# The last mode of the weights by another queue, and the last jobs dealt out earlier

## The chip, the cores and the metric

One core of a Trainium2 chip runs the whole program. The metric is the device time of one execution in microseconds (us), the median of several runs. Lower is better.

## What is computed

The first half is causal attention with a sliding window of 64, for 8 batches of 8 heads, 576 positions and 64 channels a head. The second half takes its result `x` (8 x 576 x 512) through a spectral mix and a projection:

```python
X = np.fft.rfft(x, axis=1)
Xr, Xi = np.real(X[:, :64]), np.imag(X[:, :64])
Yr = np.einsum('bmd,mde->bme', Xr, w_r) - np.einsum('bmd,mde->bme', Xi, w_i)
Yi = np.einsum('bmd,mde->bme', Xr, w_i) + np.einsum('bmd,mde->bme', Xi, w_r)
Y[:, :64] = Yr + 1j * Yi
y = np.fft.irfft(Y, n=576, axis=1)
u = x + y
out = u + np.maximum(u @ w_ch, 0.0)
```

All inputs are fp32. `w_r` and `w_i` have a 512 x 512 matrix for each of 64 modes: 134 MB together, which must all be read.

## The kernel before

**Weights.** GpSimd's queue loads the weights and converts fp32 to bf16 on the way. One load is four modes, one half of the input channels (`hb`) and one of `w_r` and `w_i` (`ri`): 128 partitions, four rows of 4 KB each in fp32, 1 MB when it has landed. `wlist` (L105 to L114) holds the order of all loads; `load_weights` (L142) issues the next ones whenever a buffer is free that `mode_half` has marked as `spent`. In the last stage the buffers are three tiles of `ringA`. The very last load is cut in three transfers, of two modes, one and one, so that products can begin before all of it has landed.

**Products by mode.** `mode_half` (L176) multiplies one load with the spectrum of `x`: eight or sixteen small matmuls at L188. In the last load (`ending`) they go mode by mode, in the order of landing. The order of the groups is written out in `steps`; the last two are `LAST` and `LAST + 1`, and the groups after number 9 are done while the loads of the second stage run, from about 200 us.

**Jobs under the loads.** Between two `mode_half` calls, TensorE works through a list of `jobs`, each of which `advance` (L613) takes in two halves: prepare, and done one call later. The first jobs multiply the transposed `x` by `w_ch` (L603, L610). When the group ahead of `LAST` is finished, 36 more are appended: `batch_job` (a batch's rows of Y: transposes at L688, products at L610), `early_u` (the inverse transform of rows that can be started without the last two groups, L715 and L716) and `add_late` (L703). `want` says how many jobs are to have been given after each `mode_half`. In the last eight halves it rises by 36 in six steps; before the last two halves all that is left is worked off.

**The tail.** When the last load has been multiplied, `finish_group` evicts its result (L627, L628), turns it (L648), and a chain of products (L1007, L1015) leads to the rows of the output: `early`, `full_u`, `full_z` and `last`, each with a buffer of `new_ut`. Its first buffer, `utx`, is 128 x 2 x 512 fp32 in a pool of its own (`utpool`, opened at L946 when the last stage starts), taken at the first use; the others are tiles of `ringA`. GpSimd adds for some rows (L835), SP and ACT send them out.

**SP's queue** has two loads at the start (L356), eight copies of a few rows of the inverse table within SBUF (`trigL` at L951, `trigLr` at L952), which the tail reads, and the output.

Of the kernel before, what the change touches and what calls it, by code (L numbers as in the profile page):

```python
# [9 lines left out]
FP32 = mybir.dt.float32  # L10
# [16 lines left out]
def kernel(  # L27
# [10 lines left out]
    nc = tc.nc  # L38
    B, H, S, D = q.shape
    NM = moe_w_r.shape[0]  # L40
    DM = moe_w_ch.shape[0]
# [7 lines left out]
    HALF = DM // 2  # L49
    NJ = 2  # L50
# [5 lines left out]
    def pool(name, bufs=1, **kw):  # L56
        opened.append(tc.alloc_tile_pool(name=name, bufs=bufs, **kw))
        return opened[-1]

    def close(*pools):  # L60
        for x in pools:
            opened.remove(x)
            x.release()

    NLB = 4
# [38 lines left out]
    wlist = []  # L104
    for at, (grp, hb) in enumerate(steps):  # L105
        for ri in range(2):
            p = 4 * grp
            if (at, ri) == ONES:
                parts = [[(p, p + 1)], [(p + 2,)], [(p + 3,)]]
            elif (at, ri) == (len(steps) - 1, 1):  # L110
                parts = [[(p, p + 1), (p + 2,), (p + 3,)]]
            else:
                parts = [[(p, p + 1, p + 2, p + 3)]]
            wlist += [(at, part, hb, ri) for part in parts]  # L114
# [15 lines left out]
        lent.update((wstart[at] + i, t) for i, t in enumerate(of))  # L130
    lentY = Yall.rearrange("p (g j) e -> p g j e", j=NJ)
    NLY = 1
    wtiles, spent = {}, set()
    held = {"a": [], "b": [], "y": []}
    room = {"a": NRA, "b": NRB, "y": NLY}
    nload = 0
# [5 lines left out]
    def load_weights(n):  # L142
        nonlocal nload
        while nload < len(wlist):
            at, parts, hb, ri = wlist[nload]
            if 2 * n <= sum(len(ps) for ps in parts):
                return
            if nload in lent:
                w = lent[nload]
            else:  # L150
                open_to = "a" if at >= 2 * EARLY else "aby" if at < EARLY + 2 else "ab"
                h = min(open_to, key=lambda h: held[h][0] if len(held[h]) == room[h] else -1)
                if len(held[h]) == room[h]:
                    if held[h][0] not in spent:
                        return
                    held[h].pop(0)
                held[h].append(nload)
                if h == "y":
                    w = lentY
                else:  # L160
                    w = {"a": ringA, "b": ringB}[h].tile([128, 4, NJ, DM], BF16, name="wi" if ri else "wr", tag="wt")
            src = moe_w_i if ri else moe_w_r
            to = 0
            for ps in parts:
                nc.gpsimd.dma_start(  # L165
                    out=w[:, to:to + len(ps)],
                    in_=src[ps[0]:ps[-1] + 1, HALF * hb:HALF * hb + HALF, :].rearrange("g (p j) e -> p g j e", j=NJ))
                for i, p in enumerate(ps):
                    wtiles[p, hb, ri] = w[:, to + i]
                to += len(ps)  # L170
            nload += 1
            n -= to

# [21 lines left out]
    with tc.manual_schedule():  # L197
# [175 lines left out]
        at = scratch[:, 3 * NTF * NM:3 * NTF * NM + NTF]  # L373
# [104 lines left out]
        for it in range(-3, NU + 3):  # L478
# [23 lines left out]
            g = starts.get(it + 2)  # L502
# [3 lines left out]
            g = starts.get(it + 1)  # L506
# [35 lines left out]
        def bank(h, shape=(128, DM), dtype=FP32, name=None):  # L542
            return banks[h].tile(list(shape), dtype, name=name or "ps" + h, tag="bank")
# [69 lines left out]
        def advance():  # L613
            if jobs:
                prepare, done = jobs.pop(0)
                pend.append((prepare(), done))
                if len(pend) < 2:
                    return
            if pend:
                tr, done = pend.pop(0)  # L620
                done(tr)
# [108 lines left out]
        def early_jobs(b):  # L730
            early_u(b, (1,))
            add_late(b, 0)
            early_u(b, (3,))
            add_late(b, 1)
            add_late(b, 2)
            early_u(b, (0, 2))
            add_late(b, 3)
# [7 lines left out]
        NT = len(tiles)  # L745
# [6 lines left out]
        def x_jobs(pl, lo, hi):  # L752
            for i in range(lo, hi):
                def done(tr, i=i):
                    XW[i] = pl.tile([128, DM], FP32R, name=f"xw{i}")
                    nc.vector.tensor_copy(out=XW[i], in_=multiply(tr))  # L756
                jobs.append((lambda i=i: transposed(tiles[i][0]), done))
# [13 lines left out]
        ps, pu = {}, {}  # L771
# [11 lines left out]
        def tail_xw(n, js=(0, 1)):  # L783
            for i in [seq[n][j] for j in js]:
                ps[i] = bank("zt"[n % 2 == 0])
                nc.tensor.matmul(out=ps[i], lhsT=ident_r, rhs=XW[i], start=True, stop=True)  # L786
# [81 lines left out]
                nc.tensor.matmul(out=ps[i], lhsT=trigIr[:, at:at + 128], rhs=zrows(b), start=False, stop=True,  # L868
                                 skip_group_check=True)

        uts, homes = {}, []
        utpool, taken_uts = None, 0
        NUT = 2 * NRA + 1

        def new_ut():
            nonlocal taken_uts
            if not homes:
                homes.append(utpool.tile([128, 2, DM], FP32, name="utx"))
            elif taken_uts == len(homes) < NUT:
                t = ringA.tile([128, 4, DM], FP32, name="ut", tag="wt")  # L880
                homes.extend([t[:, 0:2], t[:, 2:4]])
            taken_uts += 1
            return homes[(taken_uts - 1) % NUT]
# [47 lines left out]
        NX0 = 10  # L931
        x_jobs(pool("xp0", reuse_waits="tile"), 0, NX0)
        psm = None
        half = given = 0
        n0, n1 = 2 * EARLY, 4 * (NGRP - EARLY)
        for i, (grp, hb) in enumerate(steps[EARLY:]):
            f, l = grp < EARLY or hb == 0, hb == 1
            if i == EARLY:
                while tables:
                    tables.pop(0)()  # L940
                while jobs or pend:
                    advance()
                close(stmp2, yp, ringB)
                Zall = pool("zall", side="right").tile([2 * NM, B, DM], FP32R, name="Zall")
                x_jobs(pool("xp1", side="right", reuse_waits="tile"), NX0, NT)
                utpool = pool("utpool", side="right", reuse_waits="tile")  # L946
                nc.vector.memset(YT[:, :, :, rows], 0.0)
                nc.vector.tensor_scalar(out=trz.rearrange("p c g k -> p c (g k)"), scalar1=0.0, scalar2=None, op0=ALU.mult,
                                        in0=ident.unsqueeze(1).to_broadcast([128, NDCH, 128]))
                for g in range(4):  # L950
                    nc.sync.dma_start(out=trigL[32 * g:32 * g + 16], in_=trigI[rows, 0:512])  # L951
                    nc.sync.dma_start(out=trigLr.bitcast(FP32)[32 * g:32 * g + 16], in_=trigIr.bitcast(FP32)[rows, 0:512])  # L952
                given = 0
            if f:
                psm = [bank("m"), bank("m")] if grp == LAST + 1 else bank("m")
            for ri in range(2):
                if half == n0 + n1 - 2:
                    while jobs or pend:
                        advance()
                if half == n0 + n1 - 1:  # L960
                    late["first"] = bank("z")
                    late[0][1]()
                    tail_xw(0)
                mode_half(psm, grp, hb, ri, f, l)
                load_weights(len(wlist))
                while ready:
                    ready.pop(0)()
                for t in tables[0:2]:
                    t()
                del tables[0:2]  # L970
                if half == 0:
                    nc.gpsimd.dma_start(out=wch, in_=moe_w_ch.rearrange("(c p) e -> p c e", p=128))
                if l and ri:
                    finish_group(grp, psm)
                    if grp == NGRP - 1:
                        ready.pop(0)()
                        for b in range(B):
                            batch_job(b)
                            if 0 < b <= NLB:
                                early_jobs(b - 1)  # L980
                half += 1
                if half <= n0:
                    want = max(half - 4, 0) * NX0 // (n0 - 4)
                elif half <= n0 + n1 - 8:
                    want = (half - n0) * (NT - NX0) // (n1 - 8)
                else:
                    want = NT - NX0 + (half - n0 - n1 + 8) * (B + 7 * NLB) // 6
                while given < want:
                    advance()
                    given += 1  # L990
# [74 lines left out]
```

## Time and profile before

| | |
|---|---|
| median of 3 runs | 435.25 us (435.19 to 435.46) |
| profiled execution | 434.85 us, span 433.1 us |
| TensorE matmuls (PE) | 322.2 us busy, 74% |
| VectorE (DVE), ScalarE (ACT), GpSimd (POOL) | 230.0, 179.9, 101.3 us busy |
| HBM read | 163.58 MB, 400 GB/s over the span |
| chain that ended last | DMA 50%, PE 36%, issue 6% |

The engines are named as in the table; PEld is TensorE's weight load, SPq and POOLq are the queues' issues. "L188" is line 188 of the kernel before. In a line of the profile, `psm<-wi,XL` means that the tile `psm` was written from `wi` and `XL`, and `<-` behind an idle time names what ended it. A transfer's sizes are those written, so a converted load counts half of what was read. Times in a trace are from the start of the span.

### The profile page before, as it was taken

Reading aid. Unit: us, or ns where it says so; the run is one execution under the profiler, and the core shown is the slowest. Engines: PE = TensorE matmul, PEld = TensorE weight load, DVE = VectorE, ACT = ScalarE, POOL = GpSimd, SP = SyncE. Lnnn points to the kernel's source line nnn. Section 1 sums busy time; section 2 is a strip of 40 time slices with the busy share of each in tenths; the row PEclk is TensorE's granted clock in tenths of the full one; section 3 lists DMA queues with packets and bytes.
Section 4 is the critical chain, followed back from the end, with each engine's and each line's share of the span. In section 5 each row is a group of like instructions: output and inputs, shape, how many; then the busy total and the mean of one; then the engine's idle time right before and its main releaser. Section 6 shows DMA issues by size and latency. Waiting matters only on the chain.

```text
span 433.1 us, 10990 instructions
## 1 busy us (share of the span) xinstructions
PE 322.2 (74%) x4758; PEld 216.0 (50%) x4802; DVE 230.0 (53%) x472; ACT 179.9 (42%) x322; POOL 101.3 (23%) x150
## 2 busy tenths in 40 slices
PE   6888899898999999962207353767564768789994
PEld 3666667576677677641104221444343445345652
DVE  8588787876776777863104111222131315653994
ACT  5665757666666666520201100122121213325842
POOL 8322222222131231131102100012111111110990
PEclk9999999999999999996557756588899889989998
DMA  8999999999999999999999999999999999993798
GB/s 210 211 211 212 211 212 212 210 211 212 212 213 210 211 212 212 212 212 212 211 259 213 217 212 212 212 212 212 212 212 212 212 211 211 212 211 72 243 367 295
DMA packets 47280, 93.64 MB, mean 216 GB/s; under 512 B 2688, under 2 KB 3136, under 8 KB 47232
## 3 DMA queue, kind: packets, MB, share of 16 engines
q0 software_dynamic: 41008, 81.73, 99.7%
q1 hardware_dynamic: 5328, 9.77, 6.6%
q10 hardware_dynamic: 896, 1.44, 0.9%
q8 instruction: 37, 0.61, 0.5%
q14 instruction: 11, 0.09, 0.1%
HBM read 163.58 MB, written 9.44 MB: 400 GB/s over the span
## 4 chain that ended last, share of the span: by engine, by line
DMA 50%; PE 36%; issue 6%; ACT 3%; DVE 2%; POOL 1%; DVEq 0%; POOLq 0%
DMA wi<-in_moe_w_i_dram 29%; DMA wr<-in_moe_w_r_dram 22%; PE tr L231 6%; PE s L278 4%; PE s L290 3%; PE pt L298 3%; PE psm L188 3%; PE vb L243 3%; PE o L318 2%; PE s L270 2%; PE pst L786 1%; PE psz L786 1%; PE psz L610 1%; PE pst L868 1%; PE px L341 1%
## 5 line engine op out<-in xcount | busy, mean ns | idle before, releaser
L610 PE MATMUL psz<-wch,tr 128*128 128x512 f32 x176 | 62.5, 488 | 11.3 <-DMA wch<-in_moe_w_ch_dram 11.0
L756 DVE CAST xw<-psz 128x512 fp32r<-128x512 f32 x36 | 24.9, 692 | 86.1 <-PE psz L610 86.1
L584 ACT CAST tr<-ptx 128x512 fp32r<-128x512 bf16 x36 | 21.1, 586 | 102.9 <-PE ptx L603 102.9
L282 DVE TENSOR_REDUCE mx<-s 128x4 fp32r<-128x512 f32 x72 | 49.5, 688 | 26.9 <-PE s L278 26.4
L188 PEld LDWEIGHTS <-XQ 128*32 128x32 bf16 x448 | 18.9, 174 | 78.3 <-issue 53.8
L165 POOL DMA_DIRECT2D wi<-in_moe_w_i_dram x32 | 23.4, 732 | 103.6 <-PE psm L188 70.2
L188 PE MATMUL psm<-wi,XQ 128*32 128x512 bf16 x208 | 19.8, 454 | 37.1 <-DMA wi<-in_moe_w_i_dram 37.1
L610 PEld LDWEIGHTS psz<-wch,tr 128*128 128x128 f32 x176 | 37.4, 235 | 18.4 <-issue 11.6
L292 ACT ACTIVATE p<-s 128x512 bf16<-128x512 f32 x72 | 39.7, 604 | 12.8 <-PE s L290 12.8
L165 POOL DMA_DIRECT2D wr<-in_moe_w_r_dram x27 | 20.3, 754 | 95.8 <-PE psm L188 77.8
L188 PE MATMUL psm<-wr,XQ 128*32 128x512 bf16 x184 | 18.6, 483 | 28.1 <-DMA wr<-in_moe_w_r_dram 27.2
L278 PE MATMUL s<-kT,qT 64*64 64x128 bf16 (+1 forms) x576 | 29.2, 222 | 6.7 <-issue 6.7
L235 ACT COPY kT<-tr 128x576 bf16<-128x576 bf16 x32 | 23.2, 724 | 20.2 <-PE tr L231 20.2
L235 ACT COPY qT<-tr 128x576 bf16<-128x576 bf16 x32 | 23.3, 729 | 10.6 <-PE tr L231 10.6
L301 DVE COPY pts<-pt 128x1024 bf16<-128x1024 bf16 (+1 forms) x40 | 25.2, 629 | 4.5 <-PE pt L298 3.1
L278 PEld LDWEIGHTS <-qT 64*64 64x64 bf16 x576 | 17.8, 107 | 17.9 <-issue 17.5
L290 PE MATMUL s<-mx,ident_r 128*128 128x512 f32 x72 | 26.2, 437 | 0.0
L635 DVE TENSOR_TENSOR stg<-psm,Yfour 128x512 bf16<-128x512 f32 x10 | 6.9, 689 | 36.3 <-PE psm L188 36.3
L235 ACT COPY vT<-tr 128x576 bf16<-128x576 bf16 x32 | 23.3, 728 | 4.1 <-PE tr L231 4.0
L298 PE MATMUL pt<-ident_bf,p 128*128 128x128 bf16 x288 | 23.3, 221 | 1.7 <-issue 1.6
L218 POOL DMA_DIRECT2D rawk<-in_k_dram x15 | 8.1, 540 | 66.0 <-PE tr L231 59.9
L330 DVE TENSOR_TENSOR x_sb<-o,r 128x512 bf16<-128x512 f32 x32 | 22.1, 691 | 1.1
(217 smaller groups left out, 598.3 us busy)
## 6 DMA issues: line engine op xcount, KB each, us to landing
wi<-in_moe_w_i_dram POOLq DMA_DIRECT2D x29, 1024.0 KB, 18.7
wr<-in_moe_w_r_dram POOLq DMA_DIRECT2D x27, 1024.0 KB, 17.7
out_dram<-ut SPq DMA_DIRECT2D x23, 256.0 KB, 2.8
rawv<-in_v_dram POOLq DMA_DIRECT2D x16, 288.0 KB, 14.9
rawk<-in_k_dram POOLq DMA_DIRECT2D x15, 288.0 KB, 13.9
rawq<-in_q_dram POOLq DMA_DIRECT2D x15, 288.0 KB, 13.8
x_sb<-in_moe_w_r_dram POOLq DMA_DIRECT2D x2, 1024.0 KB, 15.4
out_dram<-utx SPq DMA_DIRECT2D x5, 256.0 KB, 3.1
```

The costliest lines, as they stand in the source:

```text
L165: nc.gpsimd.dma_start(out=w[:, to:to + len(ps)], in_=src[ps[0]:ps[-1] + 1, HALF * hb:HALF * hb + HALF, :].rearrange("g (p j) e -> p g j e" ...
L188: nc.tensor.matmul(out=ps[32 * g:32 * g + 32, 0:e], lhsT=of.rearrange("k s b m -> k (s b) m")[:, (3 * j + 1 - ri) * B:(3 * j + 5 - ri) * B ...
L231: nc.tensor.transpose(out=pt[ro, j, :], in_=raw[ro, TH * half + j, :], identity=ident_bf[ro, ro])
L235: nc.scalar.copy(out=to, in_=pt.rearrange("p j n -> p n j"))
L278: nc.tensor.matmul(out=s[ro, t, lo:128], lhsT=lq, rhs=kT[ro, 64 * n - 64 + lo:64 * n + 64], start=False, stop=True, skip_group_check=True)
L282: nc.vector.tensor_reduce(out=mx, in_=s, axis=AX.X, op=ALU.max, negate=True)
L290: nc.tensor.matmul(out=s, lhsT=ident_r, rhs=mx.unsqueeze(2).to_broadcast([128, 4, 128]), start=False, stop=True, skip_group_check=True)
L292: nc.scalar.activation(out=p[:, 4 * c2:4 * c2 + 4, :], in_=s, func=ACT_F.Exp, scale=EX_SCALE)
L298: nc.tensor.transpose(out=pt[:, t, :], in_=st[u]["p"][:, t, :], identity=ident_bf)
L301: nc.vector.tensor_copy(out=ps[:, 0:nt, :], in_=pt[:, 0:nt, :])
L610: nc.tensor.matmul(out=pz, lhsT=tr[:, c, :], rhs=wch[:, c, :], start=(c == 0), stop=(c == NDCH - 1))
L756: nc.vector.tensor_copy(out=XW[i], in_=multiply(tr))
```

## The change

There are two parts. The last load, whose modes are `p` to `p + 3`, is now cut in one, two and one. The first of these modes is no longer issued by GpSimd. SP loads it in fp32, in 16 transfers of 8 partitions, into `utx`, and GpSimd casts it from there into its place in the `ringA` tile, after its own last two transfers. For that, `utx` is taken at the opening of its pool, and SP's transfers are issued right there. The program's order on SP puts them behind the two loads of the start and ahead of the copies into `trigL`. The second part changes `want` in the last eight halves from 36 jobs in 6 steps to 36 in 5.5.

```diff
             elif (at, ri) == (len(steps) - 1, 1):
-                parts = [[(p, p + 1), (p + 2,), (p + 3,)]]
+                parts = [[(p,), (p + 1, p + 2), (p + 3,)]]
...
+    BY_SP = list(range(len(wlist) - 1, len(wlist)))
+    homes = []
...
             for ps in parts:
-                nc.gpsimd.dma_start(
-                    out=w[:, to:to + len(ps)],
-                    in_=src[ps[0]:ps[-1] + 1, HALF * hb:HALF * hb + HALF, :].rearrange("g (p j) e -> p g j e", j=NJ))
+                if nload in BY_SP and to == 0:
+                    own = w
+                else:
+                    nc.gpsimd.dma_start(
+                        out=w[:, to:to + len(ps)],
+                        in_=src[ps[0]:ps[-1] + 1, HALF * hb:HALF * hb + HALF, :].rearrange("g (p j) e -> p g j e", j=NJ))
...
+            if nload in BY_SP:
+                nc.gpsimd.tensor_copy(out=own[:, 0], in_=homes[0])
+                BY_SP.pop(0)
+                if BY_SP:
+                    stage_by_sp()
...
+    def stage_by_sp():
+        at, parts, hb, ri = wlist[BY_SP[0]]
+        src = (moe_w_i if ri else moe_w_r)[parts[0][0], HALF * hb:HALF * hb + HALF, :].rearrange("(p j) e -> p j e", j=NJ)
+        for p in range(0, 128, 8):
+            nc.sync.dma_start(out=homes[0][p:p + 8], in_=src[p:p + 8])
...
-            if not homes:
-                homes.append(utpool.tile([128, 2, DM], FP32, name="utx"))
-            elif taken_uts == len(homes) < NUT:
+            if taken_uts == len(homes) < NUT:
...
-                utpool = pool("utpool", side="right", reuse_waits="tile")
+                homes.append(pool("utpool", side="right", reuse_waits="tile").tile([128, 2, DM], FP32, name="utx"))
+                stage_by_sp()
...
-                    want = NT - NX0 + (half - n0 - n1 + 8) * (B + 7 * NLB) // 6
+                    want = NT - NX0 + (half - n0 - n1 + 8) * (B + 7 * NLB) * 2 // 11
```

## The prediction

> **What bounds the kernel now.** I began with the page's slices. Up to about 390 us the row of the DMA engines stands at 9 in every slice, and one queue, GpSimd's, holds them:
>
> ```profile
> DMA  8999999999999999999999999999999999993798
> ...
> q0 software_dynamic: 41008, 81.73, 99.7%
> ```
>
> Here the engines read 4 bytes for every 2 that they write, and whoever wants to end the loads earlier must take bytes off the engines that end last. So I asked second how the loads end, with a table of stages from 388 us on (its last columns: granted clock, DMA share, GB/s):
>
> ```profile
> 388.00:390.00 2.00, 1.90 (x14) 0.78 (x7) 2.00 (x4) 0.28 (x1) 0.00 (x0) 1.00 1.13 213
> 390.00:391.00 1.00, 0.64 (x8) 0.49 (x8) 0.60 (x2) 1.00 (x3) 0.00 (x0) 1.00 0.98 182
> ...
> 392.00:393.00 1.00, 1.00 (x9) 0.82 (x8) 0.52 (x2) 0.82 (x2) 0.00 (x0) 1.00 0.62 117
> 393.00:394.00 1.00, 1.00 (x6) 0.65 (x5) 0.00 (x0) 1.00 (x3) 0.00 (x0) 1.00 0.57 107
> 394.00:395.00 1.00, 1.00 (x19) 0.50 (x17) 0.00 (x0) 0.69 (x2) 0.00 (x0) 1.00 0.48 90
> 395.00:396.00 1.00, 1.00 (x11) 0.57 (x11) 0.00 (x0) 0.13 (x1) 0.00 (x0) 1.00 0.19 35
> ```
>
> A full house reads 1.13. The share falls to half (0.57) by 393 and then takes three more us to reach nothing: about eight engines are done by 392, and the other eight carry on until 396.4. The trace's landings say the same by share. The last transfer completes in sixteen parts: seven at 390.75 to 391.82, one at 393.42, eight at 394.73 to 396.38. The gap has grown slowly: 1.3 us at the first transfers, 5.0 at 190 us, 5.6 at the end. It grows by 0.6 to 1.1 us on one engine at a time, near packets of queue q8 (37 of 16 KB: instruction loading), and nearly always on one of the same eight.
>
> Third, the chain of waits around that end (start, us, what):
>
> ```profile
> 381.46 0.68 PE psm L188 x16
> 382.14 0.22 PE psp L648 x4
> 382.36 0.36 PE psy L652
> ...
> 394.51 0.60 PE psm L188 x16
> 395.11 0.32 PE psz L656
> 395.43 0.47 PE pst L786 x2
> 395.90 1.03 PE psm L188 x15
> 396.92 0.02 issue
> 396.95 0.43 DVE stg L627
> ```
>
> From 381.46 TensorE never waits for a load visibly, so it looks like TensorE's stage. But the last group of mode products takes 1.03 (1.19 from its first start), and the group of equal shape before it 0.60 (0.67): 0.4 to 0.5 us of it is a wait for the last mode. The view of the tile `wi` from 376 us dates that landing: the last issue is at 383.7, and the longest time to landing is 12.7, so 396.4.
>
> ```profile
> L165 POOL DMA_DIRECT2D wi<-in_moe_w_i_dram x3: 561/576/696, 382.5 to 383.7; - x3
> DMA to landing us min/median/max: 11.5/12.0/12.7
> ```
>
> TensorE and the slow engines thus arrive together, within half a us. A gain must move both, and the tail from 396.95 on (36 us) hangs on that point.
>
> **The change part by part.**
>
> *The mode taken off GpSimd's last transfers.* The last three transfers (2, 1, 1 modes) become two (2, 1). Loads of four modes follow each other 4.96 us apart (issues at 372.50, 377.50, 382.46), so a mode is 1.24 us on every engine. Nothing else on the eight slow engines changes, if SP's copy avoids them: the last landing goes from 396.38 to 395.14. GpSimd also issues one DMA less (0.6 us of its queue, off the path).
>
> *Where SP's 512 KB go.* SP's sixteen issues wait for the scratch of the attention stage, whose last products start at 189.3, so they run from about 190. At 0.6 us each (row of the SP issues at L951) they take 10 us; the next thing on SP is trigL at 229.79, first read at 400.27, so SP's queue hides them. A row of fp32 is 4 KB. The nearest rows are the unconverted 4.5 KB packets at the start, 178 ns, so 158 ns for 4 KB. A transfer of 8 rows has 8 packets (in the trace each row is one packet, also where a transfer has only 16 rows), so it uses at most 8 engines. If always the same eight: 16 x 158 ns and 16 completions of 22 ns, 2.9 us on each. Three cases follow. On the eight that are early, it fills part of a gap of 3 to 5 us, and they end 2.9 - 1.24 = 1.6 us later, by 395.1 at the latest: cost nothing. Spread evenly, each engine gets 1.45 us and sheds 1.24: last landing +0.2. On the eight late ones: 396.38 - 1.24 + 2.9 = 398.0.
>
> I take the first, by this reading of the trace. Its list of packets is in order of start, and where two packets start in the same nanosecond the order of the underlying table remains. A table sorted by engine would show through there. I could assign 23 such pairs of an early and a late engine between 70 and 376 us: in all 23 the early one stands first. So the early eight are probably the low-numbered ones, and I assume that a transfer too small for sixteen begins at the low end. By the Trainium skill ("DMA: Bandwidth & Descriptors", section on why a DMA increments its semaphore by 16) a transfer issued by SP runs on the largest number of engines, up to 16, that divides its outer dimension, the lowest-numbered ones, which would be 8 here; no run here shows that yet.
>
> *GpSimd's cast* (128x1024 fp32 to bf16) stands behind its last DMA issue, about 383.7. No such cast is in the trace; the nearest rows are a memset of 128x1024 bf16, 1.01 us, and two adds of 128x512 fp32, 2.5 us. Nearer by the reading of fp32 is 2.5: done by 386.3, eight us before use. It waits for all of SP's transfers, done by 210. Behind it on GpSimd stand only the adds at L835, from 401.6. Cost nothing; it would take 10 us to matter.
>
> *Jobs dealt a tenth earlier.* The order of TensorE's instructions shows what moves: one L703 product ahead of the load used at 371.54, four L610 products (1.20 us) ahead of 376.53, and a block of four L715/L716 products, four transposes L688 and one L703 ahead of 381.46. TensorE idles 0.56, 1.24 and 0.97 us at these three points, waiting for loads. The block takes 2.0 us at full clock (389 to 391, where the same block stands again) and 3.05 before, because 382.5 to 385.9 ran at half the clock:
>
> ```profile
> 381.46 0.68 PE L188 MATMUL psm<-wr,XL 128*32 128x256 bf16 x16 [0.97 <-DMA wr<-in_moe_w_r_dram]
> ```
>
> The timeline shows the third of these waits in brackets; the stage behind it, with the clock third from the end:
>
> ```profile
> 382.50:385.90 3.40, 2.93 (x10) 1.59 (x11) 0.00 (x0) 2.00 (x5) 1.77 (x3) 0.50 1.11 209
> ```
>
> Only the block crosses 381.46; the other two moves make room for it. The 2.77 us of idle take up its 2.0 but for about 0.25, by which the products of 381.46 start late. So TensorE comes 1.75 us earlier to its last group: 395.82 becomes 394.1. It also fills the quiet stretch ahead of 382.5, which is probably what the half clock followed (so did those at 338 and 352, behind stretches in which TensorE was busy for 1.33 and 0.46 us; here it was 1.92): without it TensorE gains up to 1.7 us more. What is late next is then the load. Releases that come 0.25 us later delay an issue, not a transfer: two loads of 4.96 us are always queued. The two ACT copies of L660/L663 slip behind two others, 2 us; their reader L1007 is at 398.2.
>
> *Sum.* First twelve products of the last group done by 394.7, last mode at 395.14, its products and the eviction at the old distance (396.38 to 396.95): 395.71. That is -1.24 us, and the tail shifts with it. The profiled execution took 434.85 (span 433.1 and 1.75 around it): 433.6. The median of the runs stands 0.4 above: 434.0.
>
> **The rivals.** A difference under about 0.2% (0.87 us) can't be told from none here.
>
> *No gain: the bytes only change queue.* If SP's rows spread over all engines, the last landing moves +0.2, TensorE's earlier arrival saves nothing, and the time is 435.4. For: every transfer in the trace with 16 rows or more uses sixteen. Against: 8 rows make 8 packets. The Trainium skill's rule against this change (the same page, its table of decisions) says that spreading DMAs over issuing engines gives no bandwidth because they share the sixteen engines; by it the result would be this case. The trace agrees on the average (1.13 throughout) but shows half the engines idle at the end, which that rule does not weigh.
>
> *A clock drop in the tail takes it back.* TensorE now waits for 395.14, and the stretch 392.6 to 397 holds few full products. If a window falls there as at 379 to 382.5, the next 3.4 us, which hold the serial steps L648 to L1015, run at half clock: up to +1.7, likely 1.2. Time 435.2. Against: the stretch 394.4 to 398.2 is nearly as thin before and kept its clock.
>
> *Slower: SP's rows land on the late eight.* One mechanism, decided by which engines an 8-row transfer takes: last landing 398.0, +1.6, time 436.9. For: the numbering rests on ties alone. It passes zero once a late engine takes seven of the sixteen rows that it could (1.24 / 0.18).
>
> *The load is not the limit after all* (TensorE gains only 0.45): 434.8.
>
> **How the numbers follow.** Forecast 0.61 (433.6 to 434.6 by itself: 0.3 for packet prices and as much for the tail, and a little for TensorE). No gain by spreading 0.12, clock drop 0.09, TensorE-limited 0.05: same, 0.26. Late eight 0.13. Faster by over 0.2% (below 434.4) 0.61, same 0.26, slower 0.13. The range must reach over the cases of no gain: 433.4 to 435.9, leaving out the late eight.
>
> **What would show it.** Right: the last `wi` landing near 395.1; sixteen SP transfers into `utx` near 190; the DMA share at 393 to 394 above 0.57 and nothing after 395.2; TensorE waiting for DMA at L188 near 394.5; full clock at 382.5 to 385.9; DVE L627 near 395.7. Wrong: a landing at 396.4 or later, or half clock between 396 and 400.

## The result, and the profile after

The change made the kernel slower: 437.01 us, median of 6 runs (436.07 to 438.52), beside 435.22 for the kernel before (435.09 to 435.56, 6 runs). The ratio is 1.0045, 95% interval 1.0032 to 1.0057. The forecast was 434.0 and its range ended at 435.9. Most lines stand about 16 further down in the kernel after: L627 is now L643, and the mode products of L188 are L204. GpSimd's loads went from L165 to L170, its cast is L177, and L188 is now the line of SP's transfers. The profiled execution of after took 438.52 (span 436.7), the slowest of the six. The trace thus explains a loss of 3.7 us, from 434.85 to 438.52, about twice that of the medians.

The page's slices of the kernel after (tenths of DMA busy time, GB/s) and its row of GpSimd's queue:

```profile
DMA  8999999999999999999999999999999999993798
GB/s 206 211 211 211 212 211 211 211 211 212 212 210 211 212 211 212 212 216 204 211 256 216 217 212 212 208 202 207 212 204 212 212 212 212 212 212 61 238 366 298
...
q0 software_dynamic: 40864, 81.47, 99.0%
```

The row of tenths is digit for digit that of before. Only the finer numbers show something. The queue held the engines for 99.0% instead of 99.7%, and after SP's burst (slices 18 and 19, a slice is 10.9 us) four of the five slices from 26 to 30 stand at 202 to 208, where before had 212. Some engines stood idle there.

How the loads end, by the table of stages (last columns: granted clock, DMA share, GB/s):

```profile
393.00:394.00 1.00, 0.54 (x6) 0.39 (x6) 0.00 (x0) 1.00 (x3) 0.00 (x0) 1.00 1.13 213
394.00:395.00 1.00, 1.00 (x9) 0.83 (x8) 0.84 (x2) 0.46 (x1) 0.00 (x0) 1.00 1.12 209
395.00:396.00 1.00, 1.00 (x9) 0.72 (x8) 0.62 (x2) 0.72 (x2) 0.00 (x0) 1.00 0.71 131
396.00:397.00 1.00, 1.00 (x6) 0.65 (x5) 0.00 (x0) 1.00 (x3) 0.00 (x0) 1.00 0.27 49
397.00:398.00 1.00, 1.00 (x19) 0.59 (x17) 0.00 (x0) 0.69 (x2) 0.00 (x0) 1.00 0.14 27
398.00:399.00 1.00, 1.00 (x14) 0.48 (x10) 0.00 (x0) 0.23 (x1) 0.00 (x0) 1.00 0.12 23
399.00:400.00 1.00, 0.60 (x12) 0.36 (x13) 0.00 (x0) 0.00 (x0) 0.00 (x0) 1.00 0.04 8
```

Before, the share stood at half (0.57) around 393: eight engines carried the end. Now it is full until 395 and then runs out at 0.14 and 0.12. A full house is 1.13, so 0.14 is two engines. Two engines carry the end, for three us.

The chain of waits names what the tail waits for (start, us, what), and the view of the tile `wi` dates it:

```profile
388.24 11.77 DMA wi<-in_moe_w_i_dram
400.05 0.50 PE psm L204 x3
400.57 0.44 DVE stg L643
```

```profile
L170 POOL DMA_DIRECT2D wi<-in_moe_w_i_dram x2: 571/634/698, 387.6 to 388.2; - x2
L177 POOL CAST wi<-utx x1: 1050/1050/1050, 388.8 to 388.8; 128x1024 bf16<-128x1024 f32 x1
...
DMA to landing us min/median/max: 11.2/11.5/11.8
```

The last mode landed at 400.00, 3.6 us later than before, and the eviction that the tail hangs on went from 396.95 to 400.57. GpSimd's last issues are at 387.6 to 388.2, where they were at 382.5 to 383.7. So the lateness is already in the stream when the last loads are issued.

It enters in one place. SP's burst stands between 191.9 and 200.9 us (the view of the tile `utx` between 185 and 210 us):

```profile
L188 SPq DMA_DIRECT2D utx<-in_moe_w_i_dram x16: 271/274/348, 191.9 to 200.6; - x16
```

I compared when the sixteen shares of each of GpSimd's loads complete, in both traces. Before the burst the last share of a load comes 0.3 to 0.4 us later than in the kernel before; two loads further on it comes 4.9 us later, and but for single loads it stays 4.8 to 5.0 from there on. The whole loss is there: 396.38 + 4.9 - 1.25 = 400.0.

Following each engine's chain of packets through the burst, eight chains break at its first round, six of them early engines and two late ones. Each lost 4.5 to 4.8 us for its sixteen rows. (All sixteen together lost 42.4 us, so the other eight lost some 5 between them.) One of the two late ones was the very last of all sixteen. The spread between the first share and the last went from 5.0 us to 8.7. By the end it is back at 4.9, but not because the two recovered: fourteen shares of the last load complete at 395.1 to 397.2, and the two at 399.15 and 400.00. The fourteen were held back, probably by loads that could be issued only once the two had landed; the thin slices 26 to 30 are where that shows.

### The profile page after: what moved, and what is told of

Same layout as the page of the kernel before. It is cut to its first block, busy times and chain, and to the rows that moved or that the text cites. A ratio compares the mean times of both kernels' runs of the same rounds, so it can differ in the third digit from the quotient of the medians.

```text
span 436.7 us, 11062 instructions
## 1 busy us (share of the span) xinstructions
PE 335.4 (77%) x4802; PEld 217.9 (50%) x4802; DVE 230.1 (53%) x472; ACT 180.1 (41%) x322; POOL 101.8 (23%) x150
## 4 chain that ended last, share of the span: by engine, by line
DMA 52%; PE 35%; issue 5%; ACT 3%; DVE 3%; POOL 1%; DVEq 0%; POOLq 0%
DMA wr<-in_moe_w_r_dram 33%; DMA wi<-in_moe_w_i_dram 19%; PE tr L247 5%; PE s L294 4%; PE s L306 3%; PE s L286 3%; PE pt L314 3%; PE vb L259 3%; PE psm L204 3%; PE o L334 2%; PE psz L802 1%; PE pst L802 1%; PE pst L884 1%; PE px L357 1%; ACT qT L251 1%
## 5 line engine op out<-in xcount | busy, mean ns | idle before, releaser
L626 PE MATMUL psz<-wch,tr 128*128 128x512 f32 x176 | 64.4, 500 | 11.6 <-DMA wch<-in_moe_w_ch_dram 11.0
L204 PEld LDWEIGHTS <-XQ 128*32 128x32 bf16 x448 | 18.8, 174 | 77.5 <-issue 53.8
L204 PE MATMUL psm<-wi,XQ 128*32 128x512 bf16 x208 | 21.5, 488 | 39.3 <-DMA wi<-in_moe_w_i_dram 39.3
L626 PEld LDWEIGHTS psz<-wch,tr 128*128 128x128 f32 x176 | 38.4, 241 | 19.1 <-issue 11.5
L170 POOL DMA_DIRECT2D wi<-in_moe_w_i_dram x31 | 22.9, 739 | 100.5 <-PE psm L204 71.5
L170 POOL DMA_DIRECT2D wr<-in_moe_w_r_dram x27 | 20.4, 754 | 99.3 <-PE psm L204 69.9
L204 PE MATMUL psm<-wr,XQ 128*32 128x512 bf16 x184 | 19.1, 495 | 23.4 <-DMA wr<-in_moe_w_r_dram 22.7
L286 PE MATMUL s<-mask_t,ident_bf 128*128 128x512 bf16 x72 | 28.9, 401 | 0.9 <-ACT p L308 0.7
## 6 DMA issues: line engine op xcount, KB each, us to landing
rawv<-in_v_dram POOLq DMA_DIRECT2D x16, 288.0 KB, 14.8
```

What stands on the lines that cost most here:

```text
L170: nc.gpsimd.dma_start(out=w[:, to:to + len(ps)], in_=src[ps[0]:ps[-1] + 1, HALF * hb:HALF * hb + HALF, :].rearrange("g (p j) e -> p g j e" ...
L204: nc.tensor.matmul(out=ps[32 * g:32 * g + 32, 0:e], lhsT=of.rearrange("k s b m -> k (s b) m")[:, (3 * j + 1 - ri) * B:(3 * j + 5 - ri) * B ...
L286: nc.tensor.matmul(out=s, lhsT=ident_bf, rhs=mask_t[:, mk], start=True, stop=True)
L626: nc.tensor.matmul(out=pz, lhsT=tr[:, c, :], rhs=wch[:, c, :], start=(c == 0), stop=(c == NDCH - 1))
```

## The experiments

My theory (A) was that the two late engines among the eight that SP's transfers take, and a dearer row than I had priced, are the whole of the loss. Its first rival (B) was that the loss comes from what the change does to the order of the work: the jobs dealt out earlier, the cast on GpSimd, a lower clock. The first four kernels ran on one chip, beside 19 runs of the kernel before with a median of 435.12.

**The jobs alone** (the kernel before, and this edit):

```diff
-                    want = NT - NX0 + (half - n0 - n1 + 8) * (B + 7 * NLB) // 6
+                    want = NT - NX0 + (half - n0 - n1 + 8) * (B + 7 * NLB) * 2 // 11
```

> The kernel before, with only the jobs of the last eight halves dealt out in 5.5 steps instead of 6. Theory A (SP's rows also fall on late engines: of the eight engines they use, two were among the late ones, and a row there costs more than the 0.18 us that the prediction took): the dealing out is harmless, the last load still lands at 396.4 and TensorE only waits for it, 434.8 to 435.4. Theory B (dealing out earlier costs, by waits of TensorE or a half clock in the tail): 436 to 438, with the last landing where it was.

Measured: 434.82 (434.56 to 435.21), ratio 0.9994, interval 0.9986 to 1.0003. The last mode landed at 396.37 and the eviction followed it:

```profile
396.93 0.42 DVE L627 CAST stg<-psm 128x256 bf16<-128x256 f32 x1 [6.05 <-PE psm L188]
```

TensorE does come earlier to its last group: it is busy for only 0.60 us in each us between 395 and 397. But it then waits for the same load. So the jobs cost nothing and, as long as the loads end when they did, bring at most a trace.

**SP's copy alone** (the kernel after, with that line put back to `// 6`):

> The changed kernel with the jobs dealt out in 6 steps as before. Theory A: as slow as the changed kernel, 436 to 438.5, since the last landing sets the end and is as late. Theory B: 435.2, as before.

Measured: 438.12 (436.65 to 439.32), ratio 1.0068, interval 1.0054 to 1.0082. The copy by itself is enough for the whole loss. The median is 1.1 us above that of the kernel after, though the ranges overlap. The trace shows what the earlier jobs save there. The last load is complete at 398.45, but the eviction comes 1.75 us later, where it follows 0.57 behind the load in before and after:

```profile
399.42 0.69 PE L204 MATMUL psm<-wi,XL 128*32 128x256 bf16 x16
...
400.20 0.42 DVE L643 CAST stg<-psm 128x256 bf16<-128x256 f32 x1 [3.90 <-PE psm L204]
...
384.80:388.20 3.40, 3.35 (x25) 1.56 (x25) 0.63 (x2) 0.54 (x2) 1.95 (x3) 0.50 1.12 212
```

TensorE has no wait left in the five us ahead of its last group at 399.42, and it had 3.4 us at half the clock shortly before (third from the end). In this execution the last 1.2 us are TensorE's and not the load's.

**Everything but the copy:**

```diff
-        for p in range(0, 128, 8):
-            nc.sync.dma_start(out=homes[0][p:p + 8], in_=src[p:p + 8])
+        nc.vector.memset(homes[0], 0.0)
```

> The changed kernel without SP's 16 transfers: the mode is never loaded and VectorE fills its place with zeros, so that mode's products with w_i are left out of the result. Everything else stays, the cast and the earlier jobs too. Theory A: the last landing comes to about 395.1 and the time to 433.6 to 434.2, which is what the change would give if the copy were free. Theory B, or a cost in the cast: 435 to 437 in spite of the missing transfers. A half clock in the tail would show as 435 with the landing at 395.1.

Measured: 433.93 (433.59 to 434.32), ratio 0.9969, interval 0.9958 to 0.9980. This is what the change would bring if the copy cost nothing, and it is the forecast within 0.1 us. The cast, the missing last transfer and the moved jobs are in this kernel, so B falls.

The profiled execution is the slowest of the seven, 434.32, and its loads end later than the forecast has them, at 395.97 instead of 395.14:

```profile
396.54 0.42 DVE L642 CAST stg<-psm 128x256 bf16<-128x256 f32 x1 [4.79 <-PE psm L203]
```

The last share stood 0.64 us behind that of the kernel before already ahead of 190 us, and 0.8 at the end: 396.38 + 0.8 - 1.2 = 396.0. So the mode is worth its 1.24 us. But the slowest engine's place differs between executions (in the traces of these kernels it stands between 0.3 us ahead of that of before and 0.65 behind it ahead of the burst), and that the median agrees to 0.1 us is in part luck.

**Eight transfers of sixteen rows**, to spread the copy over all engines:

```diff
-        for p in range(0, 128, 8):
-            nc.sync.dma_start(out=homes[0][p:p + 8], in_=src[p:p + 8])
+        for p in range(0, 128, 16):
+            nc.sync.dma_start(out=homes[0][p:p + 16], in_=src[p:p + 16])
```

> The changed kernel with SP's copy in 8 transfers of 16 partitions, so that every transfer uses all sixteen engines. Each late engine then takes 8 rows instead of 16 on two of them. Theory A: last landing at 396.4 - 1.24 plus 8 rows, which is +0.2 us at the prediction's price of 0.18 a row and +1.0 at the 0.28 a row that the changed kernel's trace suggests (4.5 us for 16 rows): 435.3 to 436.2, below the changed kernel. Theory B: no difference from the changed kernel, 437.

Measured: 436.73 (436.57 to 437.57), ratio 1.0041, interval 1.0029 to 1.0053. The spread between first and last share stays at 5.4 us, so the copy is indeed even; but the engines slipped by 2.7 us on the average for their eight rows, 0.34 us a row. That was more than I expected, and nearly twice what I had priced (158 + 22 ns). So there were two things to explain: which engines, and why a row was so dear.

**Which engines small transfers take** (the kernel before, with dummy transfers of 1, 2, 4 and 8 rows; `utx` is taken for them when its pool opens, as in after):

```diff
...
+                probe = moe_w_i[4 * LAST, 0:HALF, :].rearrange("(p j) e -> p j e", j=NJ)
+                at = 0
+                for rows_ in (1, 2, 4, 8):
+                    for _ in range(6):
+                        nc.sync.dma_start(out=homes[0][at:at + rows_], in_=probe[at:at + rows_])
+                        at += rows_
```

> The kernel before, with 24 extra SP transfers of 4 KB rows into utx at about 190 us that nothing reads: six of one row, six of two, six of four, six of eight. It maps which engines a small transfer takes and whether they are early or late. If a transfer of k rows runs on the k lowest engines, engine 0 gets 24 rows, engine 1 gets 18, two engines 12, four engines 6, and eight none, and the lags of the engines behind GpSimd's stream show these steps: at 0.28 us a row 6.7, 5.0, 3.4 (two), 1.7 (four), 0 (eight). Theory A (two of the eight low engines are late ones): six early engines and two late ones show a lag. Theory B (the hit engines differ from transfer to transfer): lags smeared over more than eight engines. The time is expected at 435 to 438, according to whether engine 0 or 1 is a late one.

The kernels of this and the next two ran on another chip, beside 19 runs of before at 434.93. Measured: 436.33 in the one run. Comparing the shares ahead of and behind the burst, the sixteen together lost 15.3 us for 90 rows, 0.17 us a row, and 88 of SP's 90 packets of 4 KB took 172 ns. The large steps (12 to 24 rows, 2 to 4 us) fit early engines only; the last share moved by 0.7 us, less than the step of six rows, 1.0. The traces carry no engine numbers; counted from the low end, as the prediction assumed, engines 0 to 3 looked early, and the two late ones had to be among 4 to 7. The chains overlap too much to name them. And a row could cost 0.17 us after all.

**One transfer of 128 rows:**

```diff
-        for p in range(0, 128, 8):
-            nc.sync.dma_start(out=homes[0][p:p + 8], in_=src[p:p + 8])
+        nc.sync.dma_start(out=homes[0], in_=src)
```

> After, with SP's sixteen transfers replaced by one of 128 rows, so that every engine gets eight rows and one completion. If the price is per transfer (completions, switching between transfers): 8 x 0.16 = 1.3 us an engine, last landing 396.4, time about 435.0. If it is per row and depends only on another queue's rows standing between GpSimd's (0.28 to 0.37 us a row in the two kernels so far): 2.3 to 3.0 us an engine, last landing 397.4 to 398.1, time 436.1 to 436.8. Theory A says the second.

Measured: 434.93 (434.35 to 435.46), ratio 1.0000, interval 0.9990 to 1.0009. The engines slipped by 1.3 us on the average for their eight rows, 0.165 us a row, and nearly every packet took 172 ns. I had put 436.1 to 436.8 on this kernel; that a row is dear whenever it stands between GpSimd's rows was wrong. This is the rival "the bytes only change queue" of the prediction: 1.3 us taken for 1.24 us shed.

**Half rows**, the same sixteen transfers with 2 KB packets:

```diff
+        nc.vector.memset(homes[0][:, 1:2], 0.0)
         for p in range(0, 128, 8):
-            nc.sync.dma_start(out=homes[0][p:p + 8], in_=src[p:p + 8])
+            nc.sync.dma_start(out=homes[0][p:p + 8, 0:1], in_=src[p:p + 8, 0:1])
```

> After, with SP's sixteen transfers of eight rows cut to half of each row (2 KB packets instead of 4 KB; the other half of utx is set to zero by VectorE and that half of the last mode's matrix is left out). If a row costs by its bytes: half of 4.5 us, 2.2 us on the two late engines hit, last landing about 397.4, time 435.6 to 436.1. If it costs by the packet, whatever its size: 4.5 us again, last landing 399.5 to 400, time 436.5 to 438.5.

Measured: 434.58 (433.42 to 435.95), ratio 0.9991, interval 0.9976 to 1.0006, below both of the ranges that I had put on it. All of these packets took 84 to 96 ns. Halving the bytes cut the engines' loss to less than a third of after's (11.9 us over all sixteen against 42.4). A price per transfer or per packet can't do that, nor can one that is in proportion to the bytes: the rows of 4 KB were dear because of something that half the bytes no longer reach.

**Neighbours.** A round is what one transfer has in flight at a time, one row on each engine that it takes. In the trace of after nearly all 4096 B packets of the first three rounds take 172 ns; from the fourth to the eighth round they take up to 388. The next round starts 1.5 us later, and it and the one behind it take 172 again; from there on they take up to 515. Between 190 and 210 us 211 of GpSimd's packets took over 185 ns, up to 376 (173 in the middle; in before 4 are over 185). What the transfers of 8 and of 16 rows have in common, and one transfer of 128 has not, is that rows written at the same time go to neighbouring partitions: in the single transfer each engine works through eight rows of its own. (The Trainium skill, "DMA: Bandwidth & Descriptors", section "The descriptor swizzle", gives each engine four neighbouring partitions and four more 32 further on; no trace here shows the addresses.) Two kernels test this; they and the last one ran beside 21 runs of before at 435.12. The first deals out every sixteenth row, the second does so at the source only:

```diff
-        for p in range(0, 128, 8):
-            nc.sync.dma_start(out=homes[0][p:p + 8], in_=src[p:p + 8])
+        for p in range(16):
+            nc.sync.dma_start(out=homes[0][p::16], in_=src[p::16])
```

> After, with SP's sixteen transfers of eight rows dealt out the other way: transfer i takes rows i, i+16, i+32 and so on to the same partitions of utx, where it took eight neighbouring rows. Same packets, same issues. In the profile of after the first three rounds of 4096 B packets take 172 ns and the later ones 260 to 515 ns, and GpSimd's packets beside them up to 348; with one transfer of 128 rows all took 172. Theory N (eight neighbouring rows at a time collide, at their source or at their destination): all packets 172 ns, 16 x 0.17 = 2.7 us on each engine hit, two of them late ones, last landing about 396.4 + 2.7 + 0.1 - 1.2 = 398.0, time 436.0 to 436.6. Theory S (what slows is sixteen small transfers in a row, wherever the rows lie): packets of 260 to 500 ns again, 4.5 to 5 us, 437 to 438.5.

```diff
-        for p in range(0, 128, 8):
-            nc.sync.dma_start(out=homes[0][p:p + 8], in_=src[p:p + 8])
+        for p in range(16):
+            nc.sync.dma_start(out=homes[0][8 * p:8 * p + 8], in_=src[p::16])
```

> As strided at the source (rows i, i+16, i+32 and so on), but each transfer writes eight neighbouring partitions as after does; the rows of the last mode's matrix are thereby exchanged. If the neighbouring destinations collide: 4096 B packets of 260 to 500 ns from the fourth round on, last landing 399.5 to 400, time 437 to 438.5. If the neighbouring sources collide: 172 ns throughout, last landing about 398, time about 436.3.

Measured: strided 435.49 (434.37 to 437.03), ratio 1.0015, interval 1.0002 to 1.0027; strided at the source only, 437.02 in its one run. The queues' rows in the window from 190 to 210 us (packets, MB, share of 16 engines), first of after, then of strided, then of the one strided at the source only:

```profile
q0 software_dynamic: 1840, 3.65, 101.5%
q1 hardware_dynamic: 256, 0.52, 14.8%
```

```profile
q0 software_dynamic: 1981, 3.93, 104.3%
q1 hardware_dynamic: 256, 0.52, 7.8%
```

```profile
q0 software_dynamic: 1864, 3.70, 102.6%
q1 hardware_dynamic: 256, 0.52, 13.6%
```

q1 is SP's queue. Its 256 packets (128 rows and as many completions) and its bytes are the same in all three, but they hold the engines for 14.8% of 20 us when the destinations are neighbours and for 7.8% when they are sixteen apart, whatever the source is. Beside them GpSimd moved 3.93 MB where it moved 3.65. In strided each of the 128 rows took 172 ns exactly; with only the source strided they rose to 460 again. The destination is what strided changes and the other does not. One reservation: strided also ran at a slower pace, a round each 0.62 us against 0.46 at the start of after. Pace alone is not the cause, though, since the one transfer of 128 rows ran a round each 0.32 us, over all sixteen engines, at 172 ns.

Strided came out below the 436.0 to 436.6 that I had put on it, and its last load landed at 395.99, not 398.0. Each of the eight engines hit lost 2.7 us, 0.17 us a row. But in this execution the two late ones among them stood 3.31 and 3.33 us behind the first share, 1.6 us ahead of the last; at 3.33 + 2.72 = 6.05 they moved the end by 1.1 us only.

The Trainium skill bears on this ("SBUF — State Buffer", section "Door 1: The DMA port swizzle"): four neighbouring partitions share one of sixteen ports. By it, as an estimate, a round puts four rows on each of two ports in after, four on each of four in sp16, two on each of four in strided and one on each of sixteen in the single transfer; the first two were slowed and the others not. Rows on a port are not the whole of it: the four-row transfers below put as much on one port as after's eight rows on two, and they were not slowed.

**A version that avoids both.** Four-row transfers take four engines only, by the steps of the dummy transfers early ones. Those can take sixteen rows each, so SP takes 64 rows of the mode and GpSimd the other 64 partitions:

```diff
                 if nload in BY_SP and to == 0:
                     own = w
+                    nc.gpsimd.dma_start(
+                        out=w[64:, 0],
+                        in_=src[ps[0], HALF * hb:HALF * hb + HALF, :].rearrange("(p j) e -> p j e", j=NJ)[64:])
...
-                nc.gpsimd.tensor_copy(out=own[:, 0], in_=homes[0])
+                nc.gpsimd.tensor_copy(out=own[:64, 0], in_=homes[0][:64])
...
-        for p in range(0, 128, 8):
-            nc.sync.dma_start(out=homes[0][p:p + 8], in_=src[p:p + 8])
+        for p in range(0, 64, 4):
+            nc.sync.dma_start(out=homes[0][p:p + 4], in_=src[p:p + 4])
```

> After, with SP taking only 64 rows of the last mode, in 16 transfers of four rows, GpSimd loading the other 64 partitions itself and casting 64. From the small transfers' lags (engines 0 to 3 fit early ones, two of engines 4 to 7 late ones) theory A expects four early engines to take 16 x 0.17 = 2.7 us each within their gap of 3 to 5 us, the late ones to take nothing and to shed half a mode, 0.62 us: last landing about 395.8, time 434.2 to 434.7, below both kernels. If one of engines 0 to 3 is a late one: last landing 398.4, time 436.5 to 437.

Measured: 434.35 (433.98 to 434.88, 11 runs) beside 435.12 (21 runs), ratio 0.9987, interval 0.9978 to 0.9996: faster than both kernels, by some 0.8 and 2.7 us, though the gain over the kernel before is one that this measurement can only just tell from none. SP's row in the window from 190 to 210 us, then the end of the loads and the eviction:

```profile
q1 hardware_dynamic: 128, 0.26, 3.9%
```

```profile
393.00:394.00 1.00, 1.00 (x19) 0.68 (x19) 0.00 (x0) 0.59 (x1) 0.00 (x0) 1.00 0.73 137
394.00:395.00 1.00, 1.00 (x7) 0.56 (x6) 0.00 (x0) 0.00 (x0) 0.00 (x0) 1.00 0.57 107
395.00:396.00 1.00, 0.72 (x10) 0.42 (x8) 0.00 (x0) 0.00 (x0) 0.00 (x0) 1.00 0.18 33
396.00:397.00 1.00, 0.60 (x4) 0.35 (x3) 0.20 (x1) 0.09 (x1) 0.00 (x0) 1.00 0.00 0
```

```profile
396.80 0.42 DVE L646 CAST stg<-psm 128x256 bf16<-128x256 f32 x1 [5.39 <-PE psm L207]
```

Half the rows cost just over a quarter of after's share. The last share of each load moved by 0.02 us at most across the burst (it stood 0.46 later than in the kernel before from the start in this execution, and 0.46 behind it), so the four engines that a four-row transfer takes are all early. The share of 0.73 at 393, where the kernel before had 0.57, is the early engines' gap being used. The last landing, 396.24, is 396.38 + 0.46 - 0.60: half a mode.

## Why the prediction was wrong, by its own steps

*The loads bound the kernel, through the engines that end last:* right. Without the copy the time was 433.93, and the sum had given 434.0.

*A mode is 1.24 us on every engine:* right. 396.38 + 4.9 - 1.25 in after, and 0.60 for half a mode in the last version.

*A transfer of 8 rows takes eight engines, and always the same:* right. Eight chains break at the first round, and the shares that slip keep their places from load to load.

*Those eight are the early ones:* this step failed. Six are, two are late, and in the profiled execution of after one of the two was the last of all. The 23 ties of the packet list that I counted were too thin a proof: an order that puts early ahead of late in 23 of 23 pairs doesn't say that the early eight are the lowest eight. The rule of the Trainium skill that I leaned on ("DMA: Bandwidth & Descriptors", section on why a DMA increments its semaphore by 16), the lowest-numbered engines, held in its count: eight chains for 8 rows, four for 4. Which numbers those engines have, no trace shows. Who is late I took from the ties.

*A row is 158 ns and a completion 22, 2.9 us for sixteen:* this term was mis-sized. The nearest rows came from two transfers of 128 rows at the start, and only their typical time was taken. With destinations sixteen apart the price was as I had it (172 ns a packet, 0.17 us a row); with eight neighbours at a time it was 4.5 to 4.8 us on each engine.

The two failures weigh about the same. Without any copy 433.93, with the copy strided 435.49: 1.6 us for two late engines being among the eight. With neighbouring destinations 437.01: another 1.5. Together they are the 3.0 between forecast and result. That split is an estimate, from medians of kernels whose runs scatter by 2.5 us. In the profiled execution of after, in which the very last engine was hit, the end moved by 4.5 us: 2.7 at the price of strided, and 1.8 for the dearer rows.

*The cast:* 1.05 us instead of the 2.5 that I took, in any case hidden. *SP's issues:* 16 in 8.9 us, 0.27 each instead of 0.6, hidden as said.

*The jobs:* alone they gain 0.3 us, if anything (the interval holds no change); with the load late, TensorE without them was 1.2 us late in the one trace of the copy alone. The half clock between 382.5 and 385.9 is gone, as I had thought probable (clock third from the end):

```profile
382.50:385.90 3.40, 2.02 (x8) 0.80 (x8) 3.40 (x7) 0.58 (x2) 0.68 (x1) 1.00 1.12 213
```

None of the nine traces with the earlier jobs has a half clock between 370 us and the end of the loads; of the three without, two have.

The rival "a clock drop in the tail" didn't come: the clock is 1.00 in every row of the table up to 401.

*The rival "SP's rows land on the late eight"* gave 436.9 and the right sign, and I put 0.13 on it. Its figure is close for the wrong reason: it had all the late engines at 2.9 us and a last landing at 398.0. There were two of them, at 4.5 to 4.8 us, in the profiled execution up to 400.0. Its turning point also moves: at 0.28 us a row a last engine can take four rows, not seven, before 1.24 us are used up.

What stays open: why the runs of after (436.07 to 438.52) and of strided (434.37 to 437.03) scatter over 2.5 us where the runs of the kernel before stay within 0.5 to 1.4. In the four profiled executions with a burst of eight-row transfers (after, the copy alone, strided at the source only, strided) the last share moved by 4.5, 4.4, 3.7 and 1.1 us; how far back the two late engines stand among the late when they are hit may differ from execution to execution, but only profiled ones can be followed. Open too are the numbers of the two late engines, and whether destinations alone made strided as fast as it was, since its pace was slower as well.

## What to carry to other kernels

When a stream is limited by the slowest of sixteen engines, moving bytes to another queue helps only if they land on engines that end early. Ask which ones a transfer of that many rows takes, and find out with a dummy burst and the landings of the shares, before the size is fixed: here four rows gained a little and eight lost. Price a small transfer by one of its own shape and destination beside the same stream, since 4 KB packets written to eight or sixteen neighbouring partitions at the same time cost up to twice what the same packets cost spread out.

## What was not expected of the hardware

The page's digits hid the whole loss: the DMA row is the same digit for digit, though in the kernel after fourteen of sixteen engines stood idle for nearly all of the last three us of the loads.

A 4 KB row of SP's queue beside GpSimd's converting stream took 172 ns when its fellows went to distant partitions, and up to 515 ns from the fourth round on when eight went to neighbours, up to 446 with sixteen; some of GpSimd's own packets rose from 173 to as much as 376 with them. Rows of 2 KB to eight neighbours (84 to 96 ns) and rows of 4 KB to four (172 ns but for two of 64) were not slowed.

The engines that small transfers take are not all alike: the four of a four-row transfer all ended early, and of the eight of an eight-row transfer two were among the late ones. Counted from the low end, as the prediction assumed, 0 to 3 are early and two of 4 to 7 late.
